# One 1 MB weight load in six row-strided transfers instead of one

## The chip, the cores and the metric

The kernel runs on one core of a Trainium2 chip. The metric is the time of one execution on the device in microseconds. The kernel before takes 177.71 us, the median of 3 runs (177.65 to 177.97).

## What is computed

Four tokens (batch 4, one position, width 512) pass through attention, a gated feed-forward layer, the same attention and the same feed-forward layer again, each with a layer norm without weights ahead of it and a residual sum behind it. The second pass uses the same weights and the same cache as the first.

```
q = layernorm(x) @ wq                      # 512 -> 32 heads of 128
k, v = the last 2048 positions of 8 cached heads, each used by 4 query heads
x = x + softmax(q k^T / sqrt(128)) v @ wo  # 4096 -> 512
g, u = layernorm(x) @ w_gate, layernorm(x) @ w_up   # 512 -> 1792
x = x + (sigmoid(g) * u) @ w_down
```

All inputs are bfloat16 in device memory.

## The kernel before, in words

The kernel first writes down all its operations in a plan (`_Plan.op`), with what each reads and writes as tokens. `_schedule` puts the operations of each engine into an order by modelled costs; the loads are one fixed list on the queue of the sync engine (SP) and are never reordered. `_assign_sync` then turns the dependences into semaphore waits. Loads use 24 semaphores in turn, and a load waits for the one that last used its semaphore.

On-chip memory is one large `arena` of 50 slots of 4096 bytes per partition. The K cache stays in 32 slots for both attentions; the other 18 slots pass from one weight or V block to the next. A load is put on SP as soon as a slot pair comes free in the plan (`fill`, `take_load`), and its instruction waits for the last reader of that slot. So SP's own instructions wait for compute wherever a slot is reused, and loads queue behind each other in the DMA engines otherwise.

The list of loads begins with the weight wq of the first attention: four blocks c = 0 to 3 (`load_wq(0)`, line 522), each 128 rows of 8192 bytes, one row per partition, into a slot pair. Behind them come the K blocks of 1 MB, then wo, V and K blocks alternately, then the V blocks that are left, the feed-forward weights in blocks of 448 KB and less, and wq again in halves of 512 KB. V blocks are read a second time for the second attention (behind wq), then w_gate, w_up and w_down for the last layer. In all 69.74 MB are moved.

The block c = 3 of wq is used by `q_mms` (line 793): for each half i of its columns one group of four matmuls (line 804) multiplies the normed x with each of the four blocks in turn and sums over c. The group of c = 3 is the last of each half, and `q_turn` on VectorE (line 816) follows. Then the first attention starts: VectorE transposes the K blocks in place (line 863), TensorE makes the scores (881, 892), VectorE and ScalarE the softmax (905 to 935), TensorE the product with V (982).

The second reading of wq (`load_wq(1)`) ends in the window of 116 to 125 us. Its halves come into slots that the feed-forward layer frees. Behind it the scores of the second attention (line 892) free K slots, and the V loads of the second reading go into these.

The DMA instruction of every load is at line 399, in `dma`. `load` (line 496) sets up a load of a slot pair: `left[name]` counts its uses, `emit` issues the DMA when the slot is there.

Of the kernel before, what the change touches and what calls it, by code (L numbers as in the profile page):

```python
# [254 lines left out]
class _SlotPool:  # L255
# [16 lines left out]
    bw_8k=421.0, bw_4k=409.0, bw_3k=405.0, bw_1k=347.0,  # L272
# [6 lines left out]
def build(nc, A_x, A_k, A_v, A_wq, A_wo, B_wg, B_wu, B_wd, out, cfg=None):  # L279
# [17 lines left out]
    NC = D // 128  # L297
# [15 lines left out]
    wq_d = A_wq.rearrange("(kt p) n -> p kt n", p=128)  # L313
# [9 lines left out]
    with es:  # L323
# [52 lines left out]
        def slot_ap(s):  # L376
            if s == SIDE:
                return side[:, 0:SLOT]
            return arena[:, s * SLOT:(s + 1) * SLOT]

        def stok(s, n=SLOT):
            return [("slot", s)] + (side_toks if s == SIDE else []) + ([("e", 0)] if s == SIDE and n > 1536 else [])

        def tile_ap(s):
            return arena[:, s * SLOT:(s + 2) * SLOT]

        def tok(s):
            return [("slot", s), ("slot", s + 1)]
# [7 lines left out]
        def dma(name, dst, src, w, r=(), rate="bw_4k", nbytes=None, sem=None):  # L396
            if nbytes is None:
                nbytes = dst.partition_size() * dst.free_nbytes()
            o = P.op("sync", name, 0.0, lambda e, dst=dst, src=src: e.dma_start(dst, src),
                     r=r, w=w, dma_bytes=nbytes, dma_rate=tm[rate])  # L400
            if sem is not None:
                o.sem = sem
                o.inc = 16
            return o


        loads = []
        where = {}
        left = {}
# [50 lines left out]
        def need(name):  # L460
            while name not in where:
                take_load()
            return where[name]

        def done(name):
            left[name] -= 1
            if left[name] == 0:
                s = where.pop(name)
                if name in on_free:
                    on_free[name](s)  # L470
                else:
                    pool.release(s)
                fill()
# [13 lines left out]
        def load_half(name, src, rate, size, where_):  # L487
            left[name] = 1
            homes[name] = [where_]
            on_free[name] = lambda s: hfree.add(s)  # L490

            def emit(s):
                dma(str(name), slot_ap(s)[:, 0:size], src, w=stok(s, size), rate=rate)
            loads.append((name, emit))

        def load(name, n_use, rate, part):
            left[name] = n_use

            def emit(s):
                src = part[1]  # L500
                dst = tile_ap(s)[:, 0:part[0]]
                if name[0] in ("wg", "wu"):
                    dst = tile_ap(s).rearrange("p (f n) -> p f n", f=2)[:, :, 0:F]
                elif len(src.shape) == 3 and not part[2]:
                    dst = dst.rearrange("p (f n) -> p f n", f=src.shape[1])
                dma(str(name), dst, src, w=tok(s), rate=rate)
            loads.append((name, emit))

        bounds = []
        f0 = 0  # L510
        while f0 < NFC:
# [9 lines left out]

        def load_wq(k):
            if k == 0:
                for c in range(NC):
                    load(("wq", c, k), 2, "bw_8k", (2 * SLOT, wq_d[:, c, :], False))
            else:
                for i in (1, 0):
                    for c in range(i, NC):
                        load_half(("wq", c, k, i), wq_d[:, c, i * SLOT:(i + 1) * SLOT], "bw_4k", SLOT,
                                  (((Y, 0), (Y, 1), (WQ, 1), (WQ, 0)), (None, (WQ, 0), (GA, 0), (SP, 0)))[i][c])  # L530

        def wq_part(k, c, i):

            if k == 0:
                return ("wq", c, k), i * SLOT
            return ("wq", c, k, i), 0
# [177 lines left out]
        o = P.op("scalar", "x_in", 1300.0, lambda e: e.dma_start(x_nat, x_d), w=[("prow",)])  # L714
# [78 lines left out]
        def q_mms(k, i, qb, cs):  # L793
            for c in cs:
                name, o = wq_part(k, c, i)
                s = need(name)

                src = slot_ap(s) if k else tile_ap(s)
                rd = stok(s) if k else tok(s)

                def e_q(pe, c=c, src=src, o=o):
                    last = None
                    for hh in range(4):
                        last = pe.matmul(ps[32 * hh:32 * hh + NB, qb, :], xn[:, c * NB:(c + 1) * NB],  # L804
                                         src[:, o + hh * 512:o + (hh + 1) * 512],
                                         start=(c == 0), stop=(c == NC - 1))
                    return last
                P.op("tensor", "q%d_%d_%d" % (k, i, c), 4 * tm["pe_row"], e_q,
                     r=rd + [("xn",)], w=[("qrow", i)], banks=(qb,))
                done(name)  # L810
# [15 lines left out]
        def q_first(variance):  # L826
            for n, i in enumerate((0, 1)):
                q_mms(0, i, OBS[n], range(NC))
                if n == 0:
                    variance()  # L830
                q_turn(0, i, OBS[n])

        def q_second(variance):
            q_mms(1, 1, WB, (0, 1))
            variance()
            unstash_half(tuple(named("ln_rd2Q")))
            q_mms(1, 1, WB, (2, 3))
            q_mms(1, 0, OBS[1], (0,))
            fresh.append(q_turn(1, 1, WB))
# [598 lines left out]
        stashed = ("V",) + keep[0] + (0,)  # L1438
        stay = keep[1:] + [(HKV - 2, 1)]
        load_wq(0)  # L1440
        for h in range(AHEAD):
            loads.append((("K", h), lambda _, h=h: load_k(h)))
# [7 lines left out]
        load_wo(HKV // 2 - 1)  # L1450
        load_glu(0)
        load_wq(1)
        v_tiles = {}
        n_v = 0
# [16 lines left out]
        n = len(P.ops)  # L1471
# [44 lines left out]
def bass_interleave_layers__sliding_block_cached__glu_gated_glu__decode_kernel(  # L1516
    nc, A_x, A_k_cache, A_v_cache, A_wq, A_wo, B_x, B_w_gate, B_w_up, B_w_down, out,
):
    build(nc, A_x, A_k_cache, A_v_cache, A_wq, A_wo, B_w_gate, B_w_up, B_w_down, out)
# [28 lines left out]
```

## Time and profile before

| | |
|---|---|
| median of 3 runs | 177.71 us (177.65 to 177.97) |
| profiled execution | 177.7 us |
| its span, first to last instruction | 175.9 us |
| TensorE busy | 106.1 us (60%) |
| VectorE busy | 104.2 us (59%) |
| ScalarE busy | 32.7 us (19%) |
| GpSimd busy | 21.7 us (12%) |
| data moved, mean rate | 70.00 MB, 398 GB/s |
| chain that ended last | DMA 47%, VectorE 33%, TensorE 15% |
| mean granted TensorE clock | 0.951 |

The profile is one execution. Its page lists busy time by engine, the span in 40 slices (a digit is tenths of busy time, 9 for 90% or more), the DMA queues, and the chain of work that ended last, followed back from the last instruction. In that chain a DMA piece lasts from the issue to the landing, so that a transfer that queues behind others has a long piece. Each slice is 4.4 us. The queues are q1 for the loads of SP, q10 for the x load of ScalarE, q8 and q14 for fetches of instructions. The trace behind it keeps every DMA packet (start, duration, bytes, queue) and every increment of a semaphore that ends a transfer, one by one, without the name of the DMA engine.

### The profile page before, as it was taken

To read this page: it belongs to the slowest core of one execution; us is meant where nothing else is said; L and a number is where in the kernel's file an instruction comes from. 1 tells how busy PE (TensorE), PEld (TensorE's weight loads), DVE (VectorE), ACT (ScalarE), POOL (GpSimd) and SP (SyncE) were. 2 spreads that over 40 slices of the span, in tenths; PEclk is the share of its full clock that TensorE was granted. 3 is DMA by queue.
4 is the path that set the end of the run, shared out by engine and by line. 5 is a ranking of instruction groups with operands and counts; after the bars stand their busy time and mean duration, and the time that the engine had idled before them with its cause. 6 is when DMAs were issued, how large, how long until landed. Compare 5 with 4: busy or idle time off the path is not lost.

```text
span 175.9 us, 3909 instructions
## 1 busy us (share of the span) xinstructions
PE 106.1 (60%) x1653; PEld 54.2 (31%) x1653; DVE 104.2 (59%) x256; ACT 32.7 (19%) x87; POOL 21.7 (12%) x89
## 2 busy tenths in 40 slices
PE   0536256269566282661765466547987999776663
PEld 0203112014334051340444452142322444425321
DVE  6307997994957748377322381316299999733351
ACT  2002022322303003020030000100133455430011
POOL 6100010101101001010010000000011553342000
PEclk9999999999999999999999999999999999965576
DMA  5999999999999999999999999999999999999990
GB/s 180 419 436 423 419 421 427 404 428 423 415 415 412 417 428 421 427 404 427 417 414 425 408 399 403 412 407 388 402 366 408 425 419 419 421 417 401 411 376 31
DMA packets 12738, 70.00 MB, mean 398 GB/s; under 512 B 1320, under 2 KB 1328, under 8 KB 6576
## 3 DMA queue, kind: packets, MB, share of 16 engines
q1 hardware_dynamic: 12712, 69.74, 97.4%
q8 instruction: 13, 0.21, 0.5%
q14 instruction: 5, 0.04, 0.1%
q10 hardware_dynamic: 8, 0.00, 0.0%
HBM read 69.73 MB, written 0.00 MB: 396 GB/s over the span
## 4 chain that ended last, share of the span: by engine, by line
DMA 47%; DVE 33%; PE 15%; issue 2%; SPq 1%; POOL 1%; ACT 0%; DVEq 0%
DMA arena<-in_A_v_cache_dram 19%; DMA arena<-in_B_w_down_dram 13%; DVE arena L863 12%; DMA arena<-in_A_wq_dram 10%; PE ps L892 7%; DMA arena<-in_B_w_gate_dram 5%; DVE small L905 5%; PE ps L881 2%; DVE arena L1073 2%; DVE small L909 2%; DVE side L913 2%; DVE side L940 2%; DVE arena L1078 1%; DVE arena L593 1%; DVE small L917 1%
## 5 line engine op out<-in xcount | busy, mean ns | idle before, releaser
L863 DVE STREAM_TRANSPOSE arena<-arena 128x1024 f32<-128x1024 f32 x32 | 37.0, 1205 | 0.1
L982 PE MATMUL ps<-side,arena 128*128 128x8 bf16 x576 | 18.2, 168 | 13.4 <-DMA arena<-in_A_v_cache_dram 13.4
L892 PE MATMUL ps<-arena,side 128*32 128x512 bf16 x256 | 25.2, 527 | 0.0
L982 PEld LDWEIGHTS ps<-side,arena 128*128 128x128 bf16 x576 | 16.8, 104 | 19.7 <-DMA arena<-in_A_v_cache_dram 17.2
L905 DVE TENSOR_REDUCE small<-ps 128x1 f32<-128x512 f32 x16 | 10.8, 676 | 17.6 <-PE ps L892 17.5
L920 ACT ACTIVATE side<-ps,small 128x512 bf16<-128x512 f32 x16 | 11.0, 687 | 36.7 <-PE ps L1000 18.4
L881 PE MATMUL ps<-small,msk_s 128*32 128x512 bf16 x64 | 8.6, 526 | 14.3 <-DVE arena L863 13.7
L856 ACT CAST side<-ps 128x256 bf16<-128x256 f32 x16 | 5.9, 370 | 34.7 <-PE ps L892 25.8
L892 PEld LDWEIGHTS ps<-arena,side 128*32 128x32 bf16 x256 | 8.3, 120 | 10.2 <-issue 7.5
L935 ACT CAST side<-ps 128x512 bf16<-128x512 f32 x16 | 9.4, 585 | 10.8 <-PE ps L933 10.8
L933 PE MATMUL ps<-side,perm 128*128 128x512 bf16 x16 | 8.1, 507 | 5.0 <-ACT side L920 4.9
L949 POOL CAST small<-small 128x1 bf16<-128x1 f32 x9 | 1.7, 187 | 76.2 <-ACT side L920 76.2
L804 PE MATMUL ps<-arena,xn 128*4 128x512 bf16 x60 | 7.7, 574 | 3.9 <-DMA arena<-in_A_wq_dram 3.6
L782 ACT ACTIVATE small<-ps 128x4 f32<-128x4 f32 x4 | 0.7, 173 | 47.8 <-PE ps L778 47.8
L1354 PE MATMUL ps<-arena,xn 128*4 128x448 bf16 x60 | 7.1, 530 | 3.1 <-DMA arena<-in_B_w_up_dram 1.5
L1064 PE MATMUL ps<-arena,side 128*32 128x512 bf16 x112 | 8.2, 416 | 0.2 <-DVE small L917 0.2
L940 DVE STREAM_TRANSPOSE side<-side 128x256 f32<-128x256 f32 x16 | 6.9, 433 | 2.2 <-ACT side L935 2.0
L851 PE MATMUL ps<-side,eyew 32*128 32x64 bf16 x64 | 5.6, 217 | 3.4 <-ACT side L856 2.4
L881 PEld LDWEIGHTS ps<-small,msk_s 128*32 128x32 bf16 x64 | 1.7, 98 | 17.2 <-DVE arena L863 15.8
L816 DVE STREAM_TRANSPOSE side<-ps 128x512 f32<-128x512 f32 x3 | 2.2, 717 | 8.2 <-PE ps L804 8.1
L990 DVE TENSOR_TENSOR onb<-ps,rinv 128x16 bf16<-128x16 f32 x9 | 1.7, 185 | 8.9 <-PE ps L982 8.6
L1363 DVE STREAM_TRANSPOSE side<-ps 128x448 f32<-128x448 f32 x4 | 2.5, 636 | 6.7 <-PE ps L1354 6.7
(119 smaller groups left out, 135.5 us busy)
## 6 DMA issues: line engine op xcount, KB each, us to landing
arena<-in_A_v_cache_dram SPq DMA_DIRECT2D x27, 1024.0 KB, 18.9
arena<-in_A_k_cache_dram SPq DMA_DIRECT2D x16, 1024.0 KB, 24.9
arena<-in_A_wq_dram SPq DMA_DIRECT2D x4, 1024.0 KB, 8.1
arena<-in_A_wo_dram SPq DMA_DIRECT2D x3, 1024.0 KB, 26.5
arena<-in_A_wq_dram SPq DMA_DIRECT2D x6, 512.0 KB, 6.3
arena<-in_B_w_up_dram SPq DMA_DIRECT2D x4, 448.0 KB, 6.2
arena<-in_B_w_gate_dram SPq DMA_DIRECT2D x2, 896.0 KB, 21.9
arena<-in_B_w_up_dram SPq DMA_DIRECT2D x2, 896.0 KB, 22.8
```

The source lines that it names most:

```text
L804: last = pe.matmul(ps[32 * hh:32 * hh + NB, qb, :], xn[:, c * NB:(c + 1) * NB], src[:, o + hh * 512:o + (hh + 1) * 512], start=(c == 0), s ...
L863: P.op("vector", "T%d_%d" % (h, t), c_dve(1024), lambda v, v32=v32: v.transpose(v32, v32), r=[("slot", 4 * h + t)], w=[("slot", 4 * h + t)])
L881: last = pe.matmul(ps[32 * gi:32 * gi + 32, bank, :], msk_s[:, :], msk_m[:, :].unsqueeze(1).broadcast_to([128, 256, 2]), start=True, stop= ...
L892: last = pe.matmul(ps[32 * gi:32 * gi + 32, bank, :], qbd[:, q0:q0 + 32], kt[:, cp // 2, cp % 2, jh * NJ:(jh + 1) * NJ, :], start=False, s ...
L905: lambda v: v.tensor_reduce(nmax[:, k2:k2 + 1], ps[:, bank, :], AXX, ALU.max),
L920: lambda a: a.activation(prow[:, :].rearrange("p (m x t) -> p m x t", x=32, t=2), ps[:, bank, :].rearrange("p (m t x) -> p m x t", x=32, t ...
L933: lambda pe: pe.matmul(ps[:, pb, :], perm[:, :], prow[:, :], start=True, stop=True),
L935: P.op("scalar", "pc" + tag, c_act(512), lambda a: a.copy(prow[:, :], ps[:, pb, :]), r=[("ppb", pb)], w=[("prow",)], banks=(pb,))
L940: P.op("vector", "pt" + tag, c_dve(256), lambda v: v.transpose(et, prow[:, :].bitcast(F32)), r=[("prow",)], w=[("e", k2)])
L982: last = pe.matmul(ps[:, ob, bp * 8:bp * 8 + 8], src[:, j * 128:(j + 1) * 128], ev[:, j % 2, j % 16 // 2, x0:x0 + 8], start=(j == 0), stop ...
L1064: last = pe.matmul(ps[32 * g:32 * g + 32, ob, :], ew[:, g, mq, t], src.rearrange("p (m t d) -> p t m d", t=2, d=128)[:, t], start=(n == 0) ...
L1354: last = pe.matmul(ps[32 * g:32 * g + NB, gub[n], 0:NF], xn[:, c * NB:(c + 1) * NB], slot_ap(s)[:, g * NF:(g + 1) * NF], start=(c == 0), s ...
```

## The change

The block c = 3 of the first wq is no longer loaded by `load` but by a new `load_rows`. It issues six DMAs into the same slot pair: the partitions 0, 2, 4, ... (64 rows), the partitions 1, 5, 9, ... (32 rows), and four times every sixteenth partition, from 3, 7, 11 and 15 on (8 rows each). Together they are the 128 rows, each 8192 bytes as before. The first one takes the slot pair's tokens, the others a token of their own and the same dependences. The matmul groups of c = 3 read all six tokens.

```diff
+        ROWS = ((0, 2), (1, 4)) + tuple((4 * a + 3, 16) for a in range(4))
+
+        def load_rows(name, n_use, src):
+            left[name] = n_use
+
+            def emit(s):
+                first = None
+                for n, (a, step) in enumerate(ROWS):
+                    o = dma("%s_%d" % (name, n), tile_ap(s)[a:128:step, :], src[a:128:step, :],
+                            w=[("rows", n)] if n else tok(s), rate="bw_8k")
+                    if n:
+                        o.deps.update(first.deps)
+                    else:
+                        first = o
+            loads.append((name, emit))
...
             if k == 0:
-                for c in range(NC):
+                for c in range(NC - 1):
                     load(("wq", c, k), 2, "bw_8k", (2 * SLOT, wq_d[:, c, :], False))
+                load_rows(("wq", NC - 1, k), 2, wq_d[:, NC - 1, :])
...
                 rd = stok(s) if k else tok(s)
+                if not k and c == NC - 1:
+                    rd = rd + [("rows", n) for n in range(1, len(ROWS))]
```

## The prediction

> **What bounds the kernel now.** I read the page first, then the chain of waits in order of time, then SP's timeline, and last the trace's records of single DMA packets and of the semaphore increments that end each transfer.
>
> The page's slices and its queue table:
>
> ```profile
> DMA  5999999999999999999999999999999999999990
> GB/s 180 419 436 423 419 421 427 404 428 423 415 415 412 417 428 421 427 404 427 417 414 425 408 399 403 412 407 388 402 366 408 425 419 419 421 417 401 411 376 31
> ...
> q1 hardware_dynamic: 12712, 69.74, 97.4%
> q8 instruction: 13, 0.21, 0.5%
> ...
> q10 hardware_dynamic: 8, 0.00, 0.0%
> ```
>
> The DMA engines are busy from slice 2 to slice 39 and move about 420 GB/s, so the time is a stream of 69.74 MB. It sags at slice 30 (366 GB/s, 127.5 to 131.9 us). The x load (q10) has 8 packets: four rows of data and four completions (the DMA view of the first 2.6 us counts 4 under 512 B), so a transfer of four rows runs on four engines. A transfer of 128 rows has 16 completions.
>
> The chain, in order of time:
>
> ```profile
> 2.19 11.09 DMA arena<-in_A_wq_dram
> 13.28 0.04 issue
> 13.33 0.60 PE ps L804 x4
> ...
> 63.98 22.92 DMA arena<-in_A_v_cache_dram
> ...
> 116.47 6.65 DMA arena<-in_A_wq_dram
> 123.13 0.04 issue
> 123.17 0.60 PE ps L804 x4
> ...
> 155.70 16.72 DMA arena<-in_B_w_down_dram
> 172.42 0.04 issue
> 172.47 0.60 PE ps L1395 x15
> ```
>
> The fourth wq block lands at 13.28 and starts the attention. That compute ends at 63.98 in a V load that lands only 22.92 us after its issue: it queues, so the compute before it has some 20 us of cover. The landing at 123.13 has no such cover. Compute hangs on it, and SP's timeline after it (V loads of the second read) is:
>
> ```profile
> 122.03 2.32 SPq L399 DMA_DIRECT2D arena<-in_A_v_cache_dram  x2
> 125.20 2.24 SPq L399 DMA_DIRECT2D arena<-in_A_v_cache_dram  x2
> 129.00 1.18 SPq L399 DMA_DIRECT2D arena<-in_A_v_cache_dram  x2
> 132.30 1.19 SPq L399 DMA_DIRECT2D arena<-in_A_v_cache_dram  x2
> 134.41 6.03 SPq L399 DMA_DIRECT2D arena<-in_A_v_cache_dram  x6
> ```
>
> Gaps of 0.7 to 2.1 us: here SP waits for scores, engines run dry, and that is the sag at slice 30. From 134 on the queue is full again to the end. So the end moves with the landing at 123.13, and that is set by the slowest DMA engine.
>
> The engines are not level. In the landing records the 16 completions of a transfer lie 0.46 us apart at the first block and 0.42 us at the fourth. From 33 us on they lie 1.6 us apart: at 30.76 us an instruction fetch (q8, 16 KB, 1.02 us) sits on one engine, which resumes 1.0 us late with a packet of 0.86 us. Up to 118.2 us there are eight such fetches. No spread exceeds 1.94 us, so they fell on eight different engines. For the transfer behind the landing at 123.13, eight completions lie within 0.90 us of the first and eight between 1.50 and 1.86 us.
>
> **The change part by part.** A packet of 8192 B takes 309 ns in the packet records and the next starts 3 ns before its end: 306 ns each, and a completion adds 6 ns. Now every engine carries 8 rows of the block. By the count above, 64 rows put four on each engine and 32 rows two on each. Eight rows run on eight engines, one each (between the 4 on 4 and the 128 on 16 that the trace shows), and four such transfers put four more rows on the same eight, if it is always the same eight. So eight engines (call them L) get ten packets and six completions, eight (H) six packets and two completions. L: +2 x 306 + 5 x 6 = +0.64 us. H: -612 + 6 = -0.61 us.
>
> [...]
>
> *The fourth block's landing.* L finishes 0.64 us later, so PE starts at about 13.97 instead of 13.33 and the attention with it. Hidden by the 22.92 us of the V load at 63.98. Uncovered it would cost 0.64.
>
> *SP.* Five more issues at 0.51 us each (four took 2.03): K loads issue from about 5.4 instead of 2.86. Their first packet is due when wq is done, near 13 us: hidden with 7 us to spare. The wo and V issues behind them move by as much, behind a queue of eight K loads (20 us). Semaphores are reused after 24 transfers. 22.92 us of backlog at 2.49 us per MB are 9, so that wait does not bind, shifted by five or not.
>
> *PE.* Five more waits before one L804 group, passed while the last part is still in flight: 0 to 0.2 us (0.04 each, the issue steps of the chain), at 13 us, hidden like the landing. The planner's order: bytes and rate are the same, so I cost it at nothing; DVE, ACT and POOL get no instruction.
>
> *The landing at 123.13.* Here it counts which engines are the eight late ones. If they are H, late goes from 1.86 to 1.25 and the others from 0.90 to 0.90 + 0.64 = 1.54. The last is 1.54 instead of 1.86: **-0.32 us**. If they are L, 1.86 + 0.64: **+0.64 us**. The trace names no engine. [...] I take late = H.
>
> *Behind it.* At 129.6 two leading engines ran dry, and their first packets of the next load took 2.12 and 2.06 us instead of 0.31; in the next landing those two are 0.8 us behind the other fourteen. If leaders lead 0.64 less and SP issues 0.32 earlier, they need not run dry. That is worth 0 (fetches after 133 make others late anyway: the last transfer again has eight engines 1.37 to 2.08 us behind) to 0.4. I take 0.18. Sum: -0.32 - 0.18 = **-0.5**.
>
> *Where the strided rows land.* The trace shows no load in which engines write interleaved partitions in 8 KB packets. Bounds: nothing (packets stay at 309), and double time where two engines meet (618, +306 a packet). The nearest row is the x load: two of its 1024 B packets, into partitions 0 to 3, took 44 ns each and overlapped by 37 ns, 2048 B in 51 ns or 40 GB/s, against 26.5 GB/s of one engine. So I take nothing, and keep both ends.
>
> [...]
>
> The profiled execution took 177.7 with a span of 175.9, so 1.8 lie around it, unchanged; the median of the runs is 177.71. Forecast: 177.7 - 0.5 = **177.2 us**.
>
> **Rivals.**
> - *Collision* (slower). Every packet of the six transfers at 618. L: +0.64 + 10 x 0.306 = +3.7; H: -0.61 + 6 x 0.306 = +1.23. At 123.13: max(0.90 + 3.7, 1.86 + 1.23) = 4.6 against 1.86, +2.7: **180.4**. With only the eight-row transfers meeting: 0.90 + 0.64 + 1.22 = 2.76, +0.9: 178.6. It decides once 0.90 + 0.64 + x passes 1.86, x = 0.32 us, or 341 ns a packet over ten. [...] Against it: the x rows.
> - *Wrong half.* The late eight are L, or some of each: the last engine gets +0.64, **178.35**. For it: the trace does not name engines. [...]
> - *Nothing reaches the end.* The eight rows rotate over the engines, so that no half gains, or the dry spells at 129 and 132 level the engines before the end and the gain at 123.13 is eaten by other waits of SP: **177.7**.
>
> **How the numbers follow.** Forecast 0.42 (own range 176.8 to 177.6), collision 0.33 (178.5 to 181), wrong half 0.13, nothing 0.12. About 0.2%, or 0.36 us, is what a measurement of this kernel can tell from no change: 177.35 is the edge. The forecast's gain lies between 0.1 and 0.9 and gives 0.31 faster and 0.11 same; nothing gives 0.02 faster, 0.08 same, 0.02 slower; wrong half 0.12 slower and 0.01 same; collision all slower. Faster 0.33, same 0.20, slower 0.47. The range 176.8 to 180.3 leaves out the collision above it (about 0.14) and the forecast's best end (about 0.04).
>
> **What would show it.** Right: packets of the block stay near 309 ns; 16 completions of the K loads fall into two groups 1.25 us apart from 13 us on, and near 122 us into one; the wq landing comes before 122.9; fewer first packets of 2 us near 129. Wrong: packets near 618 at 10 to 17 us and wq landing near 17 us (collision); a spread of 2.5 us at 122 (wrong half); an unchanged spread (nothing). If the fourth block's later landing shows up at 123, the cover of 22.92 us was not there.

## The result, and the profile after

The kernel after the change takes 179.69 us (median of 6 runs, 179.23 to 180.01), the kernel before 177.74 us (6 runs, 177.65 to 178.26). The ratio is 1.0106, with a 95% interval of 1.0087 to 1.0125: the change costs 1.55 to 2.2 us. The profiled span is 177.5 us instead of 175.9; the profiled execution after, 179.23 us, is the fastest of its six.

The prediction said 177.2 us. The gain of half a microsecond did not come. The time lies in the range, but that says little for the forecast: the range was wide enough for its rivals, and the time is on the side of the collision rival. In the code all lines behind the diff are 16 to 19 higher: L804 of before is L823, L892 is L911, L863 is L882, L1395 is L1414. The DMA line is still L399.

The slices and the queue table of the page after:

```profile
DMA  5999999999999999999999999999999999999990
GB/s 186 434 358 340 425 423 414 414 422 425 414 425 410 428 410 428 421 407 420 423 423 417 413 398 393 398 411 398 400 389 408 419 434 410 419 417 406 406 368 23
...
q1 hardware_dynamic: 12760, 69.74, 97.1%
```

A slice is 4.44 us here. The third and fourth (8.9 to 17.8 us) sag to 358 and 340 GB/s, where before had 436 and 423, and the engines are as busy as ever (9 in the upper row): the packets take longer, they do not wait for anything. The packet count is up by 48. That is what the prediction's count of engines gives: eight engines with five more completions, eight with one more.

How deep the sag is shows a view of busy time and rate by stretch. Its last number is GB/s, the one before it the DMA share. Before:

```profile
core 0: us, PE busy (x) PEld busy (x) DVE busy (x) ACT busy (x) POOL busy (x), PEclk, DMA share, GB/s
8.00:12.00 4.00, 2.32 (x20) 0.21 (x16) 0.00 (x0) 0.00 (x0) 0.00 (x0) 1.00 1.01 426
12.00:15.00 3.00, 1.64 (x10) 0.68 (x10) 0.79 (x2) 0.38 (x2) 0.00 (x0) 1.00 1.00 421
15.00:20.00 5.00, 1.14 (x12) 0.70 (x12) 4.86 (x7) 0.74 (x2) 0.00 (x0) 1.00 1.02 429
```

After:

```profile
8.00:12.00 4.00, 2.21 (x20) 0.21 (x16) 0.00 (x0) 0.00 (x0) 0.00 (x0) 1.00 1.05 426
12.00:15.00 3.00, 0.00 (x0) 0.00 (x0) 0.00 (x0) 0.00 (x0) 0.00 (x0) 1.00 0.98 213
15.00:20.00 5.00, 2.79 (x22) 1.42 (x22) 3.48 (x6) 1.12 (x4) 0.00 (x0) 1.00 1.01 419
```

For three microseconds all 16 engines together move 213 GB/s, half of the rate around it. In the packet records, 81 packets between 11.9 and 15.4 us take over 400 ns, in the median 618 ns, and then they come back to 309. Their excess over 309 ns is 1.6 us for each engine on average, about five packets. That stretch is the four transfers of eight rows and the first packets of the K loads beside them. The transfers of 64 and of 32 rows ahead of it ran at 309 ns on all engines.

The chain of waits after, in order of time:

```profile
5.56 9.80 DMA arena<-in_A_wq_dram
15.36 0.14 issue
15.50 0.60 PE ps L823 x4
...
66.11 22.20 DMA arena<-in_A_v_cache_dram
...
118.17 6.82 DMA arena<-in_A_wq_dram
125.00 0.04 issue
125.04 0.60 PE ps L823 x4
...
157.63 16.40 DMA arena<-in_B_w_down_dram
174.03 0.04 issue
174.07 0.60 PE ps L1414 x16
```

The fourth block lands 2.1 us later (15.36, was 13.28). The V load at 66.11 still has 22.20 us to wait, so that delay is hidden. But the wq half lands at 124.99 instead of 123.13, 1.86 later, and the last w_down block 1.6 later: what reaches the end passes through the DMA engines, not through the compute.

What the engines carry away from the stretch is seen in the landing of the next K transfer. Before, its 16 completions lie between 15.35 and 15.77 us. After, eight lie between 16.32 and 16.52 and eight between 17.34 and 17.67. The two groups of eight are the prediction's H and L, but H is 1.0 us later (forecast: 0.61 earlier) and L 1.9 later by the last completion, 2.1 by the mean of the eight (forecast: 0.64).

### The profile page after: what moved, and what is told of

Same layout as the page of the kernel before. It is cut to its first block, busy times and chain, and to the rows that moved or that the text cites. A ratio compares the mean times of both kernels' runs of the same rounds, so it can differ in the third digit from the quotient of the medians.

```text
span 177.5 us, 3920 instructions
## 1 busy us (share of the span) xinstructions
PE 105.3 (59%) x1653; PEld 54.4 (31%) x1653; DVE 104.2 (59%) x256; ACT 32.7 (18%) x87; POOL 21.7 (12%) x89
## 4 chain that ended last, share of the span: by engine, by line
DMA 46%; DVE 32%; PE 15%; SPq 2%; issue 2%; POOL 1%; ACT 0%; DVEq 0%
DMA arena<-in_A_v_cache_dram 19%; DMA arena<-in_B_w_down_dram 13%; DVE arena L882 12%; DMA arena<-in_A_wq_dram 9%; PE ps L911 7%; DVE small L924 5%; DMA arena<-in_B_w_gate_dram 5%; SPq L399 2%; PE ps L900 2%; DVE arena L1092 2%; DVE small L928 2%; DVE side L932 2%; DVE side L959 2%; DVE arena L1097 1%; DVE arena L610 1%
## 5 line engine op out<-in xcount | busy, mean ns | idle before, releaser
L882 DVE STREAM_TRANSPOSE arena<-arena 128x1024 f32<-128x1024 f32 x32 | 36.9, 1203 | 0.1
L911 PE MATMUL ps<-arena,side 128*32 128x512 bf16 x256 | 24.8, 521 | 0.1
L900 PE MATMUL ps<-small,msk_s 128*32 128x512 bf16 x64 | 8.4, 512 | 15.4 <-DVE arena L882 14.9
L911 PEld LDWEIGHTS ps<-arena,side 128*32 128x32 bf16 x256 | 8.2, 119 | 10.0 <-issue 7.2
L823 PE MATMUL ps<-arena,xn 128*4 128x512 bf16 x60 | 7.6, 574 | 6.2 <-DMA arena<-in_A_wq_dram 6.0
L1083 PE MATMUL ps<-arena,side 128*32 128x512 bf16 x112 | 7.3, 381 | 0.2 <-DVE small L936 0.2
```

Of the source, the lines that this page charges most:

```text
L882: P.op("vector", "T%d_%d" % (h, t), c_dve(1024), lambda v, v32=v32: v.transpose(v32, v32), r=[("slot", 4 * h + t)], w=[("slot", 4 * h + t)])
L900: last = pe.matmul(ps[32 * gi:32 * gi + 32, bank, :], msk_s[:, :], msk_m[:, :].unsqueeze(1).broadcast_to([128, 256, 2]), start=True, stop= ...
L911: last = pe.matmul(ps[32 * gi:32 * gi + 32, bank, :], qbd[:, q0:q0 + 32], kt[:, cp // 2, cp % 2, jh * NJ:(jh + 1) * NJ, :], start=False, s ...
L1083: last = pe.matmul(ps[32 * g:32 * g + 32, ob, :], ew[:, g, mq, t], src.rearrange("p (m t d) -> p t m d", t=2, d=128)[:, t], start=(n == 0) ...
```

## The experiments

Three theories stood at the start, all of them about the slow packets: the strided reads from device memory cost (READ), the partitions that are written cost (WRITE), or transfers of eight rows cost as such (SMALL). Later the second was refined to PORT, an assumption of the author that no trace shows directly, since the records name neither the engine nor the partition of a packet: engines that write into the same group of partitions share one write path, and the eight engines of the eight-row transfers (L) have paths in partitions 0 to 63, the other eight (H) in 64 to 127. What the runs show of it are the packet times of y1 (309 ns), y3 (606 ns) and z1 (616 ns). Its rival was COUNT: whatever eight engines get more than the others costs, wherever it goes.

### x1_three: no transfers of eight rows

```diff
-        ROWS = ((0, 2), (1, 4)) + tuple((4 * a + 3, 16) for a in range(4))
+        ROWS = ((0, 2), (1, 4), (3, 4))
```

> The block in three transfers (64, 32 and 32 rows, steps 2, 4 and 4), none of eight rows; every engine carries 8 rows. If only the eight-row transfers are slow (all three theories below): packets of the block at 309 ns, its landing at 13.3 to 13.4 us, time 177.7 within 0.3. If strided rows as such were slow: landing 1 us or more later and 178.5 or more.

Measured: 177.76 us, ratio 0.9988 (0.9962 to 1.0015). No packet from 5 to 25 us is over 400 ns, the block lands at 13.05 and the wq half at 122.91. So 64 rows of every second partition and 32 of every fourth cost nothing, nor do two more issues and waits. The whole loss is in the transfers of eight rows.

### x2_step4: eight rows of every fourth partition, inside 32 neighbours

```diff
+        ROWS = ((0, 128, 2, 0, 128, 2), (1, 128, 4, 1, 128, 4)) + tuple((32 * a + 3, 32 * a + 32, 4, 32 * a + 3, 32 * a + 32, 4) for a in range(4))
...
+                for n, (a, b, step, a2, b2, step2) in enumerate(ROWS):
+                    o = dma("%s_%d" % (name, n), tile_ap(s)[a:b:step, :], src[a2:b2:step2, :],
```

> The four eight-row transfers take every fourth partition inside 32 neighbours (3, 7, ... 31; 35, ... 63; and so on) instead of every sixteenth; rows in device memory are then 32 KB apart instead of 128 KB. Theory READ (eight engines reading rows 128 KB apart at once slow every engine's reads): packets at 309, landing near 13.9, two groups of engines 1.25 us apart, time 178.0 to 178.4 since two of the eight late engines are in the heavier half. Theory WRITE (eight engines writing partitions 16 apart share paths into the arena): better too, packets at 309 to 450, 178 to 178.8. Theory SMALL (one-row transfers are slow whatever the rows): 618 and 179.7 as in the changed kernel.

Measured: 179.61 us, ratio 1.0114 (1.0080 to 1.0148). The stretch now has 352 GB/s, and the packets tell why. The first two of the four transfers, into partitions 3 to 31 and 35 to 63, ran at 309 ns. The third, the first into the upper half, starts at about 12.5 us; its own packets still show 309 ns, but from 12.8 us on the packets of all 16 engines are slow (36 over 400 ns, median 554), until about 14.4. Each engine loses 0.58 us, about what two packets at 618 ns cost. The lower half is free, the upper is not, and the slowness shows one packet late (in z1 and y3 below, too, the first packet of the slow transfers has 309 ns). The block lands already at 14.37, but the wq half 1.4 us late: the time is as bad as after the change. So none of the three theories was right as written down: the time is that of SMALL (179.7), the packets are not, and WRITE had promised 178 to 178.8. Fewer slow packets alone do not mend the time.

### x3_dst16_src8 and x4_dst4_src16: reads and writes taken apart

Both keep the two wide transfers and change only the four of eight rows. The first writes every sixteenth partition but reads eight neighbouring rows, the second reads every sixteenth row but writes every fourth partition inside 32. Rows so come into other partitions. The lines give only the second term of `ROWS`, with the run in front.

```diff
+ x3: tuple((4 * a + 3, 128, 16, 96 + 8 * a, 104 + 8 * a, 1) for a in range(4))
+ x4: tuple((32 * a + 3, 32 * a + 32, 4, 4 * a + 3, 128, 16) for a in range(4))
```

> The destinations stay every sixteenth partition, but the four eight-row transfers read eight neighbouring rows of wq each (96 to 103, and so on), 8 KB apart; so 32 partitions get other rows of wq than the reference means, and the result is not the reference's. READ: packets at 309, landing near 13.9, 178.0 to 178.4. WRITE and SMALL: 618, landing near 15.4, 179.7 as in the changed kernel.

> The reverse: destinations every fourth partition inside 32 neighbours, sources every sixteenth row, 128 KB apart; 24 or more partitions get other rows of wq than the reference means. READ and SMALL: packets at 618, landing near 15.4, 179.7. WRITE: 309 to 450, landing 13.9 to 14.5, 178 to 178.8.

Measured: 180.08 us for the first (1.0124, 1.0098 to 1.0150) with 79 slow packets of 660 ns in the median and 224 GB/s in the stretch; 179.66 us for the second (1.0110, 1.0067 to 1.0153) with 54 slow packets of 538 ns and 314 GB/s. With neighbouring reads the stretch is as slow as after the change, so READ falls as the cause. With far reads and the written partitions of x2 it is nearer to x2 (36 slow packets, 352 GB/s) than to the change, but not the same, and WRITE's 178 to 178.8 is missed again: a smaller part of the far reads is not excluded.

### y1_low4, y2_step16, y3_high4, y4_one32: 256 KB more, in four places

Here the kernel before is left as it is, with its fourth block in one transfer of 128 rows. Right behind it come 256 KB of extra loads (wq rows, into a slot pair not yet used, read by nobody). Their partitions differ, and with them the rows that are read.

```diff
+        EXTRA = tuple((32 * (n // 2) + n % 2, 32 * (n // 2) + 32, 4) for n in range(4))
...
+                    emit(s)
+                    for n, (a, b, step) in enumerate(EXTRA):
+                        dma("extra%d" % n, tile_ap(NS - 2)[a:b:step, :], wq_d[a:b:step, NC - 1, :],
+                            r=[("slot", NS - 2), ("slot", NS - 1)], w=[("extra", n)], rate="bw_8k")
...
+ y2: tuple((4 * n + 3, 128, 16) for n in range(4))
+ y3: tuple((64 + 32 * (n // 2) + n % 2, 96 + 32 * (n // 2), 4) for n in range(4))
+ y4: ((3, 128, 4),)
```

> The kernel before plus four loads of eight rows (256 KB in all, their data unused, the result unchanged) right behind the unchanged fourth wq block; destinations every fourth partition inside 0 to 31 and 32 to 63. PORT (an engine's write path serves a fixed group of partitions, and eight-row transfers run on the eight engines that own partitions 0 to 63): each engine stays in its own half, packets stay at 309 ns, eight engines get 4 x 0.31 = 1.25 us more, eight none; K0 lands in two groups 1.25 us apart; the end +0.3 if the late eight at 111 us are all of the other half, +1.0 to 1.3 if one or two of them are of this half: 178.0 to 179.0. COUNT (any eight-row transfer costs what after paid, wherever it writes): packets near 618 behind the block, +1.9 us, 179.6.

> As the low-half kernel, but the four extra loads write every sixteenth partition, from 3, 7, 11 and 15 on, as the changed kernel does; the 128-row block itself is unchanged. Data unused, result unchanged. PORT: four of the eight rows of each lie in 64 to 127, on paths that the other eight engines also use for K0: 618 ns packets on all engines for 3 to 4 us, eight engines +2.5 us, the other eight +0.9 to 1.2; the end +1.9 to 2.5, 179.6 to 180.3. COUNT: the same as the low-half kernel within 0.3 us.

> As the low-half kernel, but the four extra loads write every fourth partition inside 64 to 95 and 96 to 127. Data unused, result unchanged. PORT: all their packets meet those of the other eight engines: 618 ns on both while they last (2.5 us), eight engines +2.5, the other eight +1.25; the end +1.9 to 2.5, 179.6 to 180.3, and K0's two groups 1.2 us apart but both later than in the low-half kernel. COUNT: the same as the low-half kernel within 0.3 us.

> The kernel before plus one load of 32 rows (256 KB, the same bytes as in the other three; every fourth partition from 3 on) behind the unchanged fourth wq block. Data unused, result unchanged. PORT and COUNT alike: two more packets on each of 16 engines at 309 ns, +0.62 us for all, no new spread: the end +0.6, 178.4. If it costs as much as the four eight-row loads into the low half, the bytes and not the imbalance are what those pay for.

Measured, against 177.60 us of before: y1 179.55 (1.0101, 1.0060 to 1.0142), y2 180.94 (1.0182, 1.0140 to 1.0224), y3 180.57 (1.0149, 1.0110 to 1.0187), y4 178.55 (1.0045, 1.0023 to 1.0067). The same stretch, the last column is GB/s; y1, the low half:

```profile
12.00:15.00 3.00, 1.65 (x10) 0.68 (x10) 0.92 (x2) 0.38 (x2) 0.00 (x0) 1.00 1.00 418
```

y2, every sixteenth partition:

```profile
12.00:15.00 3.00, 1.43 (x10) 0.68 (x10) 0.71 (x1) 0.25 (x2) 0.00 (x0) 1.00 1.08 273
```

y3, the high half:

```profile
12.00:15.00 3.00, 1.43 (x10) 0.68 (x10) 0.70 (x1) 0.24 (x2) 0.00 (x0) 1.00 1.01 270
```

The same bytes, in the same number of transfers, of the same step in y1 and y3: 309 ns a packet where eight engines write partitions 0 to 63, a median of 606 ns on all engines where they write 64 to 127, and of 654 ns where they write both (packets that start between 13 and 15 us). PORT as expected, COUNT's equal packets fall.

But y1's time is the one that COUNT had written down (179.6) and outside PORT's 178.0 to 179.0. It has no slow packet at all in the stretch, its two groups of K landings are 15.26 to 15.59 and 16.72 to 16.90 us, so H is in time and L 1.1 us late, and that reaches the end. Its chain of waits at the wq half:

```profile
117.57 6.84 DMA arena<-in_A_wq_dram
124.41 0.04 issue
124.45 0.59 PE ps L813 x2
```

124.41 instead of 123.13, +1.28 us. If all eight late engines of the prediction were H, L's 0.90 + 1.25 = 2.15 against 1.86 would make that landing 0.3 us later; 178.0 was written down for that case. It is 1.28 later, and the end 1.8 (1.1 to 2.5): some of the late engines are L. The bytes themselves are no excuse, since y4 moves the same 256 KB on all 16 engines for 0.8 us (0.4 to 1.2).

### y5_next8: eight neighbouring partitions

```diff
+        EXTRA = tuple((8 * n, 8 * n + 8, 1) for n in range(4))
```

> As the low-half kernel, but each of the four extra eight-row loads writes eight neighbouring partitions (0 to 7, 8 to 15, 16 to 23, 24 to 31). Data unused, result unchanged. HALVES (an engine only has to stay in its half of the partitions): 309 ns, eight engines +1.25 us, the time of the low-half kernel, 179.5. GROUPS OF FOUR (four neighbouring partitions are one write path, shared by whoever writes there): four engines on a path, 4 x 309 = 1236 ns a packet on the eight engines, +4.9 us for them, the other eight undisturbed at 309; 182 to 183.5. GROUPS OF EIGHT: all eight on one path, up to 2.5 us a packet, +9.9 us, above 185.

Measured: 182.22 us, ratio 1.0265 (1.0212 to 1.0319). The time is in the range of groups of four, the picture is not. The stretch:

```profile
12.00:15.00 3.00, 1.10 (x10) 0.64 (x10) 0.37 (x1) 0.00 (x0) 0.00 (x0) 1.00 1.06 232
```

The packets that start between 13 and 15 us take about 770 ns (most of them 761 to 801), not 1236, and they do so on all engines: H, which carried none of the extra rows, lands the next K transfer at 17.36 to 17.73 us (15.26 to 15.59 in y1). So these transfers hold up engines that carry none of their rows. None of the three pictures that were written down beforehand had that. It bears on the change as well: there only four of the eight rows of a transfer go into the upper half, so by PORT they can meet at most four of the eight engines of H on one path, and yet all 16 engines slow down to about 618 ns. How much of that is shared paths and how much this holding up, the runs do not separate. y5 also reads neighbouring rows, but x3 did so too, at 660 ns. HALVES falls in any case: the low half alone does not make a transfer free (about 770 ns), its rows have to be spread as in y1 (309 ns).

### z1_halves: two transfers of 64 neighbouring rows

```diff
+        ROWS = ((0, 64), (64, 128))
...
+                for n, (a, b) in enumerate(ROWS):
+                    o = dma("%s_%d" % (name, n), tile_ap(s)[a:b, :], src[a:b, :],
```

> The fourth wq block in two transfers of 64 neighbouring partitions (0 to 63, then 64 to 127), nothing strided, 16 engines in each. Result unchanged. PORT (write paths belong to groups of partitions, half of the paths are in each half): two engines on each path, 618 ns a packet on all 16 engines over the block, all engines +2.4 us with no new spread, block landing near 15.7 and the wq half near 125.5; 180.0 to 180.4. IMBALANCE ONLY (what costs is that eight engines get more packets): 309 ns, no change, 177.7.

Measured: 179.94 us, ratio 1.0126 (1.0086 to 1.0167). No stride, 16 engines in each transfer and no imbalance, and still:

```profile
8.00:12.00 4.00, 2.16 (x20) 0.21 (x16) 0.00 (x0) 0.00 (x0) 0.00 (x0) 1.00 1.03 338
12.00:15.00 3.00, 0.00 (x0) 0.00 (x0) 0.00 (x0) 0.00 (x0) 0.00 (x0) 1.00 0.99 216
15.00:20.00 5.00, 2.79 (x22) 1.42 (x22) 3.28 (x6) 1.12 (x4) 0.00 (x0) 1.00 1.01 415
```

134 packets, in the median 616 ns. The block lands at 15.56, the next K transfer in one group (17.72 to 18.02 us, 2.3 later than before), the wq half at 125.72. This is the plainest of the runs: 16 engines that write into one half of the partitions have half of the rate (216 GB/s against 421 before, 616 ns a packet against 309), whichever half, and a later transfer does not make up for it.

### z2_late_start: only the compute is late

```diff
                 rd = stok(s) if k else tok(s)
+                if not k and c == NC - 1:
+                    need(("K", 0))
+                    rd = rd + tok(0)
```

> The loads as before, but the matmul groups of the fourth wq block also wait for the first K transfer (15.8 us), so that the attention starts 2.5 us or more later with the DMA stream unchanged. Result unchanged. COVERED (the landing at 13.28 is hidden behind the queue of loads): 177.7, within 0.3, wq half still landing at 123.1. NOT COVERED: +2.5, 180.2, which would put the cost of the change on the late landing and not on the engines.

Measured: 177.51 us, ratio 0.9996 (0.9976 to 1.0015). Its chain of waits:

```profile
2.91 12.69 DMA arena<-in_A_k_cache_dram
15.73 0.60 PE ps L807 x4
...
65.29 21.45 DMA arena<-in_A_v_cache_dram
...
116.22 6.78 DMA arena<-in_A_wq_dram
```

The matmuls start at 15.73, 0.2 us later than after the change, and the end does not move. The late landing of the fourth block is covered, as the prediction had it; the loss is in the engines.

### z3_low_only: eight rows only where they are free

```diff
+        ROWS = ((0, 128, 2), (1, 128, 4), (3, 32, 4), (35, 64, 4), (67, 128, 4))
...
+                for n, (a, b, step) in enumerate(ROWS):
+                    o = dma("%s_%d" % (name, n), tile_ap(s)[a:b:step, :], src[a:b:step, :],
```

> The changed kernel with its eight-row transfers kept in the lower half: even partitions (64 rows), partitions 1, 5, ... (32), 3 to 31 and 35 to 63 in steps of four (8 each), 67 to 127 in steps of four (16 rows on 16 engines). Result unchanged. PORT: eight engines 9 packets and the others 7 in place of 8 and 8; the eight-row packets at 309, the 16-row packets and whatever meets them at 618 for one packet; eight engines +0.6, the others about 0; 178.3 to 178.8, about 1 us better than the changed kernel. If the number of transfers or the strides cost as such: 179.5.

Measured: 178.37 us, ratio 1.0028 (1.0001 to 1.0055), as expected: five transfers and strides, 18 slow packets instead of 81, the last K landing at 16.08 us (0.3 late), the wq half 0.6 late. It is better than the change and no better than before. No kernel here beats the kernel before.

### The runs side by side

Landings in us later than before; the K column is the last completion of the first K transfer (15.77 before), the wq column the wq half in the chain (123.13 before).

| run | K | wq half | ratio of the times |
|---|---|---|---|
| x1_three | -0.2 | -0.2 | 0.9988 |
| z2_late_start | -0.2 | -0.1 | 0.9996 |
| z3_low_only | 0.3 | 0.6 | 1.0028 |
| y4_one32 | 0.5 | 0.7 | 1.0045 |
| x2_step4 | 1.0 | 1.4 | 1.0114 |
| y1_low4 | 1.1 | 1.3 | 1.0101 |
| x4_dst4_src16 | 1.3 | 2.1 | 1.0110 |
| the change | 1.9 | 1.9 | 1.0106 |
| x3_dst16_src8 | 2.2 | 2.2 | 1.0124 |
| y3_high4 | 2.2 | 2.5 | 1.0149 |
| z1_halves | 2.3 | 2.6 | 1.0126 |
| y2_step16 | 2.5 | 2.7 | 1.0182 |
| y5_next8 | 3.4 | 3.1 | 1.0265 |

Differences of 0.2 us mean nothing here: the third wq block, which is the same in all kernels, lands at 10.79 before and at 10.57 to 10.77 in the others (11.10 in x3).

What the last engine loses at 16 us it still has lost at 123 us, in every run (x4 adds 0.8 on the way). The time follows to within its interval in all but two: x2 (1.4, at the lower edge) and y5, whose 3.1 us stand against 3.8 to 5.7 in the median; its profiled execution, the fastest of four, is 3.2 above before.

The leaders do not keep what they gain. After, the 16 completions of a transfer are 2.70 us apart at 113 us and 1.69 at 119 us, since the engines in front run dry between 110 and 112 us (two first packets take 1445 and 926 ns). The other runs with more than 2.7 us at that point end at 1.7 to 2.3, too. Before, with 1.9 us, none runs dry there.

## Why the prediction was wrong, step by step

*Where the strided rows land: "I take nothing, and keep both ends".* This step failed. The price was the other end, 618 ns, for the four transfers of eight rows and for what ran beside them; for the wide transfers it was nothing. The nearest row misled: two packets of 1024 B of the x load that overlap, 40 GB/s together, say little about full packets of 8192 B. In z1, 2 x 8192 B in 616 ns are 26.6 GB/s, the rate of one engine alone at 309 ns (26.5), as if two engines had to share it.

The runs decide against the x rows: four transfers of eight rows into partitions 64 to 127 have 606 ns a packet (y3), the same into 0 to 63 have 309 ns (y1). PORT agrees with both; which engine wrote which partition they do not show. That every packet of all six transfers would be slow, as the collision rival had it, did not come either (309 ns in the two wide ones).

*"H: -0.61 us".* This failed too, and with it the gain. H did carry six packets instead of eight, but the engines of H were slowed beside L's rows: 1.0 us late instead of 0.61 early, a difference of 1.6 or about five packets at +309 ns. What the prediction did not see is shown by y3 and y5: eight-row transfers on L into partitions 64 to 127 slow the packets of all engines (606 ns, against 309 ns in y1), and so do those into eight neighbouring partitions of the low half (about 770 ns), H included, which carries none of their rows. Taking rows off H did not take their cost off it.

*"L: +0.64 us".* The count was right (48 more packets in the queue table, two groups of eight), the size was not: with the 1.6 us of slow packets that each engine had it is 0.64 + 1.6 = 2.2, and 2.1 was measured by the mean of the eight, 1.9 by the last. H comes out of the same sum: -0.61 + 1.6 = 1.0. The prediction's rival had priced all ten packets of L as slow, +3.7; about five were, the eight-row transfers and a K packet behind them. Its smaller version, "only the eight-row transfers meeting", gave 178.6 because it kept the late eight in H.

*"I take late = H".* This failed as well, and -0.32 with it: no run shows that the late eight are H, since the trace names no engine, and what the runs show in its place is a mixture. In the completions after, where the two groups are 1.0 us apart from 16 us on, five of the first seven fetches take an engine out of H and two an engine out of L. In y1, without a slow packet, the wq half is 1.28 us late, which no late engine in H explains. Of the 16 completions that make up the landing at 125.00, the two L engines with a fetch are at 124.77 and 124.82, so nearly all of L's delay reaches it (+1.7). The last, at 125.00, is the engine of the eighth fetch (120.46 us); to which group it belongs these readings do not settle.

*The fourth block's landing, SP, PE, the planner: nothing.* Right. z2 starts the attention at 15.73 and costs nothing. SP's issues took longer than the 0.51 us that were taken, and were hidden:

```profile
0.79 5.33 SPq L399 DMA_DIRECT2D arena<-in_A_wq_dram  x9
6.17 5.15 SPq L399 DMA_DIRECT2D arena<-in_A_k_cache_dram  x8
```

The K loads issue from 6.17 (forecast 5.4), and their first packets are due near 12 us. PE starts 0.14 us behind the landing, inside the 0 to 0.2 that was given.

*"Behind it": -0.18.* Not there. Two first packets of 1.55 and 2.07 us near 131 us remain (2.12 and 2.06 before): two engines run dry as before.

*The landing at 123.13 has no cover.* Right, and it is the reason why 1.9 us lost at 16 us end as 1.95 in the median time (1.5 in the profiled execution): the runs in the table move with it.

So the sum was sound and three of its terms were not. With 1.6 us of slow packets on every engine and late engines in L it would have read 177.7 + 2.2 = 179.9, against 179.69; that is worked out after the result, with sizes taken from it.

## What to carry to other kernels

A transfer that runs on fewer engines than the stream around it has to be asked two things: which partitions it writes (309 ns a packet in y1, 606 in y3, about 770 in y5), and which of its engines is last at the next landing that has no cover. Rows moved from one engine to another slowed the packets of all 16 here (618 ns against 309), so the stream could not be levelled in this way. A block that fills all 128 partitions in one transfer, or in wide strided ones, ran at full rate (309 ns, before and x1); halves of neighbouring partitions ran at half (616 ns, z1).

## What the runs showed of the hardware

- Sixteen engines that write 64 neighbouring partitions take 616 ns for a packet of 8192 B, and 309 ns where the same number of rows is spread over all 128 (z1 against the 64-row transfer of x1).
- Transfers of eight rows can slow engines that carry none of their rows: in y5 the packets of H take the same 770 ns or so as those of L, and in y1, with every fourth partition of the low half, 309 ns. What the engines share is not shown by these runs, nor why the packet time was 770 ns and not 1236.
- A delay of the last engine of 0.3 to 3.4 us at 16 us is still there at 123 us. The lead of the engines in front is not: where it grew to 2.7 us and more by 113 us, they ran dry and 1.7 to 2.3 us were left at 118 us.
- A fetch of instructions of 16 KB, of which the kernels before and after have 13 each, takes 0.88 to 1.25 us of one DMA engine before and 0.93 to 1.11 us after. After each of the first seven in the changed kernel, one of the 16 completions comes about 1.5 us later than it did, and it stays late in the transfers that follow.
